# A Mamba-2 scan with a hash-routed expert layer: x in two transfers per sequence, y in natural order, C's parity masks on ScalarE, and a new order of the steps

## The chip, the cores and the metric

The kernel runs on one NeuronCore of a Trainium2 chip. Five engines take part: TensorE (PE, with its weight loads as PEld), VectorE (DVE), ScalarE (ACT), GpSimd (POOL) and SyncE (SP), which here only issues DMAs. The metric is the device time of one launch in microseconds. Before the change it was 355.7 us, the median of three runs (354.11 to 358.03).

## The reference

Two stages follow one another, all in float32.

The first is a state-space scan over 4 sequences, 8 heads, 768 steps, with 32 values per head (x) and a state of 16 (B and C). With `la = log(clip(a, 1e-6, 1))` and chunks of 32 steps:

```python
cum = np.cumsum(la, axis=-1)
L = np.exp(cum[:, :, :, None] - cum[:, :, None, :]) * causal
M = np.einsum('bhin,bhjn->bhij', Cc, Bc) * L
y = einsum('bhij,bhjd->bhid', M, xc) + einsum('bhin,bhnd->bhid', Cc, state) * exp(cum)
state = exp(sum(la)) * state + sum_j Bc_j xc_j exp(cum[-1] - cum_j)
```

The second takes the result as 3072 tokens of 256 values. A token's expert is `token_ids * 2654435761 % 8`; each expert computes `relu(x @ w1[e]) @ w2[e]` with a hidden width of 1024.

## The kernel before

**The scan.** A sequence is cut into 12 units of 64 steps; two units make a chunk of 128 steps, so there are 6 chunks per sequence and 24 in all (`gc` counts them, `b, c = divmod(gc, 6)`). `fac` holds exp(-cum) and exp(cum), with cum counted from the middle of a unit, for all four sequences.

For a sequence `b` the steps are these. `load_bc` and `load_x` read B, C and x. `rows(b, 0)` multiplies B by its factor and `rows(b, 1)` C by its own. `put_steps` stores the scaled B to a scratch tensor in HBM, and `get_steps` reads it back as the tile `bs` with steps on the partitions. `turn_b` and `turn_c` transpose the scaled B and C on PE, 96 rows at a time, into `bt` and `ct`; `turn_c` also makes `ce` (two copies of C, each with the heads of one parity masked to zero) and `cp` (C times the decay of a unit). `states` multiplies `bs` by x on PE and chains the units' states on DVE; `blocks` spreads the states into `up`. `grams` forms C·B for a chunk and multiplies it by the causal mask on DVE, giving `m`; `outputs` adds `cp`·`up` and `m`·x in PSUM, ACT copies the sum to `y_sb`, and SP stores it to `y_tokens` in HBM.

**What sets the order.** `tc.manual_schedule()` keeps each engine's instructions in the order of the code, so every engine, and SP as the queue of the loads and stores, works through one fixed list. Lines 490 to 504 are the prologue for sequence 0. In the loop of lines 506 to 541 chunk `gc` issues `grams(gc + 1)` and `outputs(gc)`, then one segment of `routing()` (a generator, advanced by `next(todo)`), and then a step for the next sequence `nb`, chosen by `c`:

```python
c == 0: rows(nb, 0), rows(nb, 1), load_x(nb + 1)
c == 1: put_steps(nb), turn_b(nb), load_bc(nb + 1)
c == 2: get_steps(nb), turn_c(nb)
c == 3: states(nb, 0)
c == 4: states(nb, 1), blocks(nb, 1, UH + 1)
c == 5: blocks(nb, UH + 1, NU)
```

**The routing.** Its first segment makes the expert ids from the token ids (`eid_i`, `eid_r`, a PE transpose), the second a one-hot mask and two PE matmuls that count tokens, the next three prefix sums; later ones build `at` and `of`, whose product on PE (`L346`, 24 matmuls) inverts the permutation into `idx_in` and `idx_out`.

**The expert stage.** After the last chunk GpSimd gathers token rows by `idx_in`, PE runs the eight experts, and GpSimd scatters the results.

**Buffers.** The pool `ps_t` has two PSUM tiles named `tp`, used by the transposes, `states`, the routing and `steps`; `ps_y` has one `y_ps`. `spin` is a run of matmuls whose result is not read. `aload` holds three `x_t` and one `bc`.

Of the kernel before, what the change touches and what calls it, by code (L numbers as in the profile page):

```python
# [20 lines left out]
def kernel(  # L21
# [65 lines left out]
    def load_bc(b):  # L87
        t = aload.tile([NR, 2, H, RS, NS], F32, name="bc", bufs=1)
        for i, src in ((0, B), (1, C)):
            nc.sync.dma_start(out=t[:, i].rearrange("p h r n -> p h (r n)"),  # L90
                              in_=src[b].rearrange("h (p r) n -> p h (r n)", r=RS))
        bcs[b] = t

    def load_x(b, parts=1):

        t = aload.tile([P, NU, G, D], F32, name="x_t", bufs=3)
        for u in range(parts):
            us = slice(u * NU // parts, (u + 1) * NU // parts)
            for h in range(H):
                q, k = divmod(h, G)  # L100
                nc.sync.dma_start(out=t[q * HL:(q + 1) * HL, us, k],  # L101
                                  in_=x[b, h].rearrange("(u j) d -> j u d", j=HL)[:, us])
        xs[b] = t

    load_bc(0)
# [3 lines left out]
    load_x(0, 2)  # L109
# [3 lines left out]
    def load_w(e):  # L113
# [10 lines left out]
    upto = const.tile([P, P], F32)  # L124
    nc.gpsimd.affine_select(out=upto, in_=ones, pattern=[[1, P]], compare_op=OP.is_ge,
                            fill=0.0, base=0, channel_multiplier=-1)
    causal = const.tile([P, 2 * G, RS, RU], F32)
    nc.gpsimd.memset(causal[0:HL], 1.0)
    nc.gpsimd.affine_select(out=causal[0:HL], in_=causal[0:HL], pattern=[[0, 2 * G], [1, RS], [RS, RU]],
                            compare_op=OP.is_ge, fill=0.0, base=0, channel_multiplier=-1)  # L130
    nc.gpsimd.tensor_copy(out=causal[HL:P], in_=causal[0:HL])
# [42 lines left out]
    nc.vector.tensor_scalar(out=a_t, in0=a_t, scalar1=1e-6, scalar2=1.0, op0=OP.max, op1=OP.min)  # L174
# [5 lines left out]
    tot = apre.tile([NR, BH], F32)  # L180
    nc.vector.tensor_copy(out=tot, in_=cum[:, :, RS - 1])
    rel_ps = ps_t.tile([P, 512], F32, name="tp")
    nc.tensor.matmul(out=rel_ps[0:NR, 0:BH], lhsT=rel_w.rearrange("p k r -> p (k r)"), rhs=tot, start=True, stop=True)
    off = apre.tile([NR, BH], F32)
    nc.vector.tensor_copy(out=off, in_=rel_ps[0:NR, 0:BH])
    nc.vector.tensor_tensor(out=cum, in0=cum, in1=off.unsqueeze(2).to_broadcast([NR, BH, RS]), op=OP.add)
    fac = apre.tile([NR, 2, BH, RS], F32)
    nc.scalar.activation(fac[:, 0], cum, AF.Exp, scale=-1.0)
    nc.scalar.activation(fac[:, 1], cum, AF.Exp)
# [5 lines left out]
    nc.gpsimd.tensor_copy(out=totx, in_=tot.unsqueeze(2).to_broadcast([NR, BH, NS]))  # L195

# [162 lines left out]

# [23 lines left out]
    def turned(b, i):  # L383
        t = rws.pop((b, i))
        for r0 in (0, RS // 2):
            tp = ps_t.tile([P, 512], F32, name="tp")
            v = tp[:, 0:RS // 2 * NR].rearrange("p (r c) -> p r c", c=NR)
            for r in range(RS // 2):
                nc.tensor.transpose(out=v[:, r], in_=t[:, r0 + r], identity=ident[0:NR, 0:NR])  # L389
            yield r0, v.rearrange("p r (k c) -> p r k c", c=RU)  # L390

    def turn_b(b):
        bt = abat.tile([P, NU, RU, RS], F32, name="bt")
        for r0, v in turned(b, 0):
            o = bt[:, :, :, r0:r0 + RS // 2].rearrange("p k c r -> p r k c")
            if b == 0 and r0:
                nc.vector.tensor_copy(out=o, in_=v)
            else:
                nc.scalar.activation(o, v, AF.Copy)
        bts[b] = bt  # L400

    def turn_c(b):
        ct = abat.tile([P, NU, RS, RU], F32, name="ct", bufs=1)
        for r0, v in turned(b, 1):
            nc.scalar.activation(ct[:, :, r0:r0 + RS // 2].rearrange("p k r c -> p r k c"), v, AF.Copy)
        ce = abat.tile([P, 2, NU, HL], F32, name="ce")
        c3 = ct.rearrange("p k r c -> p k (r c)")
        for e in range(2):
            nc.vector.tensor_scalar(out=ce[:, e], in0=c3, scalar1=par[:, e:e + 1], scalar2=None, op0=OP.mult)  # L409
        cp = abat.tile([P, NU, HL], F32, name="cp")  # L410
        nc.gpsimd.tensor_tensor(out=cp, in0=c3, in1=step[:, b].unsqueeze(2).to_broadcast([P, NU, HL]), op=OP.mult)
        ces[b], cps[b] = ce, cp

    def states(b, half):
# [6 lines left out]
        for i in range(n):  # L421
            k = half * UH + i
            for r in range(G):
# [3 lines left out]
                                 rhs=xb[w, k, 2 * g:2 * g + 2].rearrange("p h d -> p (h d)"), start=True, stop=True)  # L427
# [8 lines left out]
    def blocks(b, k0, k1):  # L436
# [4 lines left out]
        nc.gpsimd.tensor_tensor(out=ups[b][:, k0:k1], in0=sts[b][:, k0:k1].unsqueeze(2).to_broadcast(sh),  # L441
# [4 lines left out]
    def grams(gc):  # L446
# [3 lines left out]
        for u in range(2):  # L450
            for r in range(G):
# [3 lines left out]
                                 lhsT=bts[b][rr, 2 * c + u].rearrange("p c r -> p (c r)"), rhs=ces[b][rr, :, 2 * c + u],  # L455
# [3 lines left out]
                                in1=causal.rearrange("p (g x) r c -> p g (x r c)", g=2), op=OP.mult)  # L459
        ms[gc] = m  # L460

    def outputs(gc):
# [11 lines left out]
        for h in range(G):  # L474
            g, e = divmod(h, 2)
            for q in range(2):
                w = slice(q * HL, (q + 1) * HL)
                for u in range(2):
                    k = 2 * c + u
                    nc.tensor.matmul(out=y_ps[u * HL:(u + 1) * HL, q, h * D:(h + 1) * D], lhsT=m[w, g, u, e],  # L480
                                     rhs=xs[b][w, k, h], start=(k == 0 and h == 0), stop=(h == G - 1),
# [3 lines left out]
        for u in range(2):  # L485
            t0 = gc * P + u * HL
            nc.sync.dma_start(out=y_dram[t0:t0 + HL, :].rearrange("(p r) d -> r p d", r=RS),
# [235 lines left out]
```

## Time and profile before

| | us |
|---|---|
| median of 3 runs | 355.7 |
| the profiled execution | 356.14 |
| its span in the trace | 354.4 |
| PE busy | 287.9 (81%) |
| DVE busy | 111.6 (31%) |
| ACT busy | 49.4 (14%) |
| POOL busy | 110.0 (31%) |
| mean granted PE clock | 0.834 |

The profile is one execution; 1.74 us of its time lie outside the span. Times of single instructions are counted from the span's start. A busy PE is not PE at its peak: the granted clock says which of its two levels (1.2 and 2.4 GHz, 0.5 and 1.0) it ran at. The scan takes the first 127 us of the span, the gathers follow, and the expert stage runs from 142.8 us to the end.

### The profile page before, as it was taken

The page shows a single profiled execution, that of the slowest core. Times are in us where ns is not written, and L with a number is a line of the kernel's source. Part 1 is how long each engine was busy: PE and PEld are TensorE (multiplying, and loading weights), DVE is VectorE, ACT ScalarE, POOL GpSimd, SP SyncE. Part 2 cuts the span into 40 slices and gives each one's busy share as a digit, 9 for nine tenths or more (in the row PEclk, how much of TensorE's full clock was granted, in tenths as well). Part 3 has the DMA queues.
Part 4 walks back from the last instruction along what each step waited for, and adds up shares of the span by engine and source line. Part 5 has one row for each costly group of instructions (what it writes and reads, how often), then busy time and mean ns, then how long its engine had stood idle before and what let it go on. Part 6 is the DMA issues. An engine that isn't in the chain of part 4 may idle for free.

```text
span 354.4 us, 6033 instructions
## 1 busy us (share of the span) xinstructions
PE 287.9 (81%) x2461; PEld 182.5 (51%) x2461; DVE 111.6 (31%) x222; ACT 49.4 (14%) x101; POOL 110.0 (31%) x115
## 2 busy tenths in 40 slices
PE   6743789818777722999999999999999999999940
PEld 5533668617566620555555555555555555655510
DVE  2724359745958301111221221121222212211110
ACT  4200211300211010100110111111111111111110
POOL 8404315212616317413054052161350310201330
PEclk9855555656757885699999999999999999999985
DMA  8598841591944459403415324424210000100010
GB/s 129 104 158 114 191 95 30 99 213 35 297 109 151 147 157 372 154 10 129 147 44 167 118 74 140 135 78 168 99 59 5 30 14 0 46 0 15 33 35 14
DMA packets 58129, 36.45 MB, mean 103 GB/s; under 512 B 36559, under 2 KB 53993, under 8 KB 58100
## 3 DMA queue, kind: packets, MB, share of 16 engines
q1 hardware_dynamic: 55284, 29.49, 32.2%
q0 software_dynamic: 2816, 6.56, 5.7%
q8 instruction: 20, 0.33, 0.4%
q14 instruction: 9, 0.07, 0.1%
HBM read 28.17 MB, written 8.13 MB: 102 GB/s over the span
## 4 chain that ended last, share of the span: by engine, by line
PE 45%; issue 20%; DMA 14%; DVE 9%; POOL 5%; SPq 4%; ACT 1%; POOLq 0%; ACTq 0%; DVEq 0%
PE h_ps L595 16%; PE o_ps L604 15%; DMA out_dram<-o_sb,idx_out 6%; DMA bs<-b_steps 3%; DVE st L433 3%; POOL out_dram L565 3%; PE y_ps L480 2%; PE gram L454 2%; PE tp L426 2%; DMA xg<-y_tokens,idx_in 2%; SPq L101 2%; PE xt_ps L583 2%; DMA bc<-in_C_dram 2%; PE tp L389 1%; PE y_ps L471 1%
## 5 line engine op out<-in xcount | busy, mean ns | idle before, releaser
L595 PE MATMUL h_ps<-xT,w 128*128 128x416 f32 x256 | 102.3, 524 | 0.3 <-DVE xT L584 0.3
L604 PE MATMUL o_ps<-hT,w 128*128 128x416 f32 x256 | 102.1, 518 | 0.0
L604 PEld LDWEIGHTS o_ps<-hT,w 128*128 128x128 f32 x256 | 47.5, 190 | 40.1 <-issue 36.3
L565 POOL DMA_INDIRECT out_dram<-o_sb,idx_out x32 | 31.2, 974 | 114.1 <-ACT o_sb L626 95.8
L595 PEld LDWEIGHTS h_ps<-xT,w 128*128 128x128 f32 x256 | 47.4, 195 | 32.5 <-issue 30.8
L560 POOL DMA_INDIRECT xg<-y_tokens,idx_in x32 | 32.0, 1000 | 50.2 <-PE xt_ps L583 20.4
L590 DVE TENSOR_SCALAR hT<-h_ps 128x416 f32<-128x416 f32 x32 | 18.9, 592 | 74.8 <-PE h_ps L595 74.8
L584 DVE COPY xT<-xt_ps 128x256 f32<-128x256 f32 (+1 forms) x32 | 12.0, 375 | 77.6 <-PE xt_ps L583 77.6
L588 ACT ACTIVATE hT<-h_ps 128x416 f32<-128x416 f32 x32 | 16.6, 517 | 100.6 <-PE h_ps L595 100.6
L426 PE MATMUL tp<-x_t,bs 64*32 64x64 f32 x352 | 13.3, 308 | 17.0 <-issue 10.4
L441 POOL TENSOR_TENSOR up<-st,own 128x768 f32<-128x768 f32 (+1 forms) x8 | 13.4, 1672 | 44.2 <-DVE st L433 44.2
L454 PE MATMUL gram<-ce,bt 32*64 32x128 f32 x384 | 23.3, 379 | 2.2 <-DVE ce L409 2.2
L480 PE MATMUL y_ps<-x_t,m 64*64 64x32 f32 x768 | 21.4, 257 | 4.2 <-DVE m L458 4.2
L480 PEld LDWEIGHTS y_ps<-x_t,m 64*64 64x64 f32 x768 | 21.6, 184 | 5.1 <-DVE m L458 5.1
L583 PE MATMUL xt_ps<-ident,xg 128*128 128x128 f32 (+1 forms) x64 | 12.6, 280 | 13.0 <-DMA xg<-y_tokens,idx_in 12.0
L583 PEld LDWEIGHTS xt_ps<-ident,xg 128*128 128x128 f32 (+1 forms) x64 | 8.4, 147 | 26.2 <-issue 23.0
L484 ACT ACTIVATE y_sb<-y_ps 128x256 f32<-128x256 f32 x24 | 9.2, 384 | 89.5 <-PE y_ps L480 86.2
L458 DVE TENSOR_TENSOR m<-gram,causal 128x512 f32<-128x512 f32 x24 | 16.4, 685 | 16.4 <-PE gram L454 16.4
L426 PEld LDWEIGHTS tp<-x_t,bs 64*32 64x32 f32 x352 | 10.6, 164 | 18.7 <-issue 16.4
L454 PEld LDWEIGHTS gram<-ce,bt 32*64 32x64 f32 x384 | 15.0, 184 | 5.3 <-DVE ce L409 2.4
L471 PE MATMUL y_ps<-up,cp 64*64 64x128 f32 x176 | 14.4, 384 | 3.4 <-POOL up L441 2.7
L626 ACT ACTIVATE o_sb<-ot_ps 128x256 f32<-128x256 f32 x16 | 6.1, 384 | 60.2 <-PE ot_ps L623 60.2
(121 smaller groups left out, 192.8 us busy)
## 6 DMA issues: line engine op xcount, KB each, us to landing
w<-in_moe_w_dram SPq DMA_DIRECT2D x16, 1024.0 KB
y_tokens<-y_sb SPq DMA_DIRECT2D x48, 64.0 KB
x_t<-in_x_dram SPq DMA_DIRECT2D x24, 96.0 KB
bc<-in_B_dram SPq DMA_DIRECT2D x4, 384.0 KB
bc<-in_C_dram SPq DMA_DIRECT2D x4, 384.0 KB
b_steps<-rows SPq DMA_DIRECT2D x4, 384.0 KB
bs<-b_steps SPq DMA_DIRECT2D x8, 192.0 KB
x_t<-in_x_dram SPq DMA_DIRECT2D x16, 48.0 KB
```

The lines of the kernel that those rows point to most:

```text
L426: nc.tensor.matmul(out=tp[32 * r:32 * r + 32, i * PW:(i + 1) * PW], lhsT=bs[w, k, 32 * g:32 * g + 32], rhs=xb[w, k, 2 * g:2 * g + 2].rearr ...
L454: nc.tensor.matmul(out=gram[q * HL:(q + 1) * HL, g, u * P:(u + 1) * P], lhsT=bts[b][rr, 2 * c + u].rearrange("p c r -> p (c r)"), rhs=ces[ ...
L458: nc.vector.tensor_tensor(out=m.rearrange("p g u e i -> p g (u e i)"), in0=gram[:, :, 0:2 * P], in1=causal.rearrange("p (g x) r c -> p g ( ...
L471: nc.tensor.matmul(out=y_ps[u * HL:(u + 1) * HL, q, 0:P], lhsT=cps[b][w, k], rhs=ups[b][w, k].rearrange("p g x -> p (g x)"), start=True, s ...
L480: nc.tensor.matmul(out=y_ps[u * HL:(u + 1) * HL, q, h * D:(h + 1) * D], lhsT=m[w, g, u, e], rhs=xs[b][w, k, h], start=(k == 0 and h == 0), ...
L560: nc.gpsimd.indirect_dma_start(out=dst, out_offset=None, in_=y_dram[:], in_offset=bass.IndirectOffsetOnAxis(ap=idx, axis=0), bounds_check= ...
L565: st = nc.gpsimd.indirect_dma_start(out=out[:], out_offset=bass.IndirectOffsetOnAxis(ap=idx, axis=0), in_=src, in_offset=None, bounds_chec ...
L583: nc.tensor.transpose(out=tp[:, i, 0:r], in_=g[0:r, i * P:(i + 1) * P], identity=ident[0:r, 0:r])
L588: nc.scalar.activation(o, i, AF.Relu)
L590: nc.vector.tensor_scalar_max(out=o, in0=i, scalar1=0.0)
L595: nc.tensor.matmul(out=hp, lhsT=w1s[e][:, i, f * P:(f + 1) * P], rhs=xT[e][:, i], start=(i == 0), stop=(i == DP - 1))
L604: nc.tensor.matmul(out=oP[e][:, j, 0:CAP], lhsT=w2s[e][:, f, j * P:(j + 1) * P], rhs=h, start=(f == 0), stop=(f == FP - 1))
```

## The change

- `load_x` issues two transfers per sequence, one for each group of four heads, instead of 8 (16 for sequence 0), and the tile's free dimensions are `[head, unit, value]` instead of `[unit, head, value]`. The runs of contiguous bytes stay 32 floats long.
- The transposes write PSUM as `(column, row)`, so that `bt`, `ct`, `ce` and `causal` hold a unit's 64 steps in natural order; `outputs` stores a chunk with one transfer of 128 rows instead of two of 64 permuted rows.
- `turn_c` makes `ce` with four ScalarE activations per sequence, each with a scale per partition, straight from PSUM; the two DVE multiplications go.
- In the prologue: `tok` is loaded before B and C; `upto` and `causal` are built on GpSimd after `totx`; `tot` is a view and not a copy; `rel` is added straight from PSUM; the first five segments of `routing()` are issued before chunk 0; `rows(0, 1)`, `cp` and the first state block of sequence 0 are on DVE; `grams(0)` stands ahead of the spins.
- In the loop: `put_steps` moves from `c == 1` to `c == 0`, `get_steps` from `c == 2` to `c == 1`; `load_bc` moves to `c == 0`, `load_x` to `c == 1`, behind `get_steps`; `blocks` follow their `states` directly.

```diff
 def load_bc(b):
-    t = aload.tile([NR, 2, H, RS, NS], F32, name="bc", bufs=1)
+    t = aload.tile([NR, 2, H, RS, NS], F32, name="bc")
...
-def load_x(b, parts=1):
-    t = aload.tile([P, NU, G, D], F32, name="x_t", bufs=3)
-    for u in range(parts):
-        us = slice(u * NU // parts, (u + 1) * NU // parts)
-        for h in range(H):
-            q, k = divmod(h, G)
-            nc.sync.dma_start(out=t[q * HL:(q + 1) * HL, us, k],
-                              in_=x[b, h].rearrange("(u j) d -> j u d", j=HL)[:, us])
+def load_x(b):
+    t = aload.tile([P, G, NU, D], F32, name="x_t", bufs=3)
+    for q in range(2):
+        nc.sync.dma_start(out=t[q * HL:(q + 1) * HL].rearrange("j h k d -> j (h k) d"),
+                          in_=x[b, q * G:(q + 1) * G].rearrange("h s d -> (h s) d").rearrange("(c j) d -> j c d", j=HL))
...
 def turned(b, i):
...
-        v = tp[:, 0:RS // 2 * NR].rearrange("p (r c) -> p r c", c=NR)
+        v = tp[:, 0:RS // 2 * NR].rearrange("p (c r) -> p c r", r=RS // 2)
         for r in range(RS // 2):
-            nc.tensor.transpose(out=v[:, r], in_=t[:, r0 + r], identity=ident[0:NR, 0:NR])
+            nc.tensor.transpose(out=v[:, :, r], in_=t[:, r0 + r], identity=ident[0:NR, 0:NR])
...
-def turn_c(b):
-    ct = abat.tile([P, NU, RS, RU], F32, name="ct", bufs=1)
-    for r0, v in turned(b, 1):
-        nc.scalar.activation(ct[:, :, r0:r0 + RS // 2].rearrange("p k r c -> p r k c"), v, AF.Copy)
-    ce = abat.tile([P, 2, NU, HL], F32, name="ce")
-    c3 = ct.rearrange("p k r c -> p k (r c)")
-    for e in range(2):
-        nc.vector.tensor_scalar(out=ce[:, e], in0=c3, scalar1=par[:, e:e + 1], scalar2=None, op0=OP.mult)
+def turn_c(b, eng):
+    ct = abat.tile([P, NR, RS], F32, name="ct", bufs=1)
+    ce = abat.tile([P, 2, NR, RS], F32, name="ce")
+    for rs, v in turned(b, 1):
+        for e in range(2):
+            nc.scalar.activation(ce[:, e, :, rs], v, AF.Identity, scale=par[:, e:e + 1])
+        nc.scalar.activation(ct[:, :, rs], v, AF.Copy)
...
-        for u in range(2):
-            t0 = gc * P + u * HL
-            nc.sync.dma_start(out=y_dram[t0:t0 + HL, :].rearrange("(p r) d -> r p d", r=RS),
-                              in_=y_sb[u * HL:(u + 1) * HL].rearrange("p q d -> p (q d)"))
+        nc.sync.dma_start(out=y_dram[gc * P:(gc + 1) * P, :], in_=y_sb.rearrange("p q d -> p (q d)"))
...
+todo = iter(routing())
+next(todo)
 rows(0, 0, nc.vector)
 put_steps(0)
+rows(0, 1, nc.vector)
+heads()
 get_steps(0)
-rows(0, 1, nc.gpsimd)
-heads()
+load_bc(1)
+load_x(1)
 turn_b(0)
 steps()
+next(todo)
+turn_c(0, nc.vector)
+grams(0)
 spin(ones, 2)
-load_bc(1)
-turn_c(0)
+next(todo)
+next(todo)
+next(todo)
 spin(ones, 4)
-grams(0)
 states(0, 0)
-blocks(0, 1, UH + 1)
-load_x(1)
-todo = iter(routing())
+blocks(0, 1, 2, nc.vector)
+blocks(0, 2, UH + 1, nc.gpsimd)
...
         if c == 0:
             rows(nb, 0, nc.gpsimd)
             rows(nb, 1, nc.gpsimd)
+            put_steps(nb)
+            if nb + 1 < NB:
+                load_bc(nb + 1)
+        elif c == 1:
+            turn_b(nb)
+            get_steps(nb)
             if nb + 1 < NB:
                 load_x(nb + 1)
-        elif c == 1:
-            put_steps(nb)
-            turn_b(nb)
-            if nb + 1 < NB:
-                load_bc(nb + 1)
         elif c == 2:
-            get_steps(nb)
-            turn_c(nb)
+            turn_c(nb, nc.gpsimd)
         elif c == 3:
             states(nb, 0)
+            blocks(nb, 1, UH + 1, nc.gpsimd)
         elif c == 4:
             states(nb, 1)
-            blocks(nb, 1, UH + 1)
+            blocks(nb, UH + 1, NU, nc.gpsimd)
```

SP's list from the first chunks of sequence 1 on, where sequence 2 is prepared; before:

```order
L487 DMA y_tokens<-y_sb 8x8x256 x4
L101 DMA x_t<-in_x_dram 64x12x32 x8
L487 DMA y_tokens<-y_sb 8x8x256 x2
L373 DMA b_steps<-rows 96x1024
L90 DMA bc<-in_B_dram 96x8x128
L90 DMA bc<-in_C_dram 96x8x128
L487 DMA y_tokens<-y_sb 8x8x256 x2
L379 DMA bs<-b_steps 64x12x64 x2
```

And after:

```order
L477 DMA y_tokens<-y_sb 128x256 x2
L368 DMA b_steps<-rows 96x1024
L90 DMA bc<-in_B_dram 96x8x128
L90 DMA bc<-in_C_dram 96x8x128
L477 DMA y_tokens<-y_sb 128x256
L374 DMA bs<-b_steps 64x12x64 x2
L98 DMA x_t<-in_x_dram 64x48x32 x2
```

The eight x transfers that stood ahead of the store and the two reads of the scaled B now stand behind them, as two, and B and C of the following sequence still lie between the store and the reads.

PE's list in the prologue (`L168`/`L157` are the spins, `L389`/`L385` the transposes, `L426`/`L418` the states); before:

```order
L389 MATMUL tp<-ident,rows 128x96 x8
L200 MATMUL tp<-step_w,totx 128x12 x4
L168 MATMUL y_ps<-ones,ident 128x128 x2
L389 MATMUL tp<-ident,rows 128x96 x8
L168 MATMUL y_ps<-ones,ident 128x128 x4
L454 MATMUL gram<-ce,bt 64x128 x8
L426 MATMUL tp<-x_t,bs 32x64 x24
```

And after:

```order
L239 MATMUL tp<-ident,eid_r 128x24
L385 MATMUL tp<-ident,rows 128x96 x8
L196 MATMUL tp<-step_w,totx 128x12 x4
L250 MATMUL tp<-mask,ones 128x192
L251 MATMUL tp<-mask,upto 128x192
L385 MATMUL tp<-ident,rows 128x96 x8
L446 MATMUL gram<-ce,bt 64x128 x8
L157 MATMUL y_ps<-ones,ident 128x128 x6
L418 MATMUL tp<-x_t,bs 32x64 x24
```

The routing's three matmuls now come before the first states, and all six spins directly ahead of them.

DVE's list around the first `rows`; before:

```order
L186 TENSOR_TENSOR cum<-cum,off 96x256
L223 CAST iota_b<-iota_c 128x53
L368 TENSOR_TENSOR rows<-bc,fac 96x8x8x16
L209 TENSOR_REDUCE par<-hm 128x2
L210 TENSOR_TENSOR hm<-hm 128x4
```

And after:

```order
L174 TENSOR_TENSOR rel<-cum,tp 96x256
L219 CAST iota_b<-iota_c 128x53
L235 TENSOR_SCALAR eid_i<-tok 24x128
L237 CAST eid_r<-eid_i 24x128
L363 TENSOR_TENSOR rows<-bc,fac 96x8x8x16 x2
L205 TENSOR_REDUCE par<-hm 128x2
```

The scaled B still stands behind `iota_b`, which waits for GpSimd's `iota_c`, and now behind the two expert-id instructions too.

## Rows read from the trace of the kernel before

**Rows 1.** Stages: length, busy us of PE, PEld, DVE, ACT, POOL, clock, DMA share, GB/s

```profile
30.10:59.20 29.10, 21.86 (x433) 18.12 (x437) 16.43 (x38) 4.62 (x9) 9.05 (x6) 0.50 0.54 113
59.20:88.40 29.20, 19.00 (x440) 15.72 (x444) 17.56 (x35) 4.85 (x10) 8.13 (x5) 0.59 0.53 108
88.40:111.60 23.20, 18.88 (x440) 15.31 (x440) 18.70 (x26) 4.75 (x10) 9.05 (x6) 0.63 0.55 164
111.60:127.20 15.60, 11.12 (x340) 9.20 (x340) 5.77 (x15) 2.30 (x6) 6.95 (x3) 0.89 0.53 177
127.20:354.40 227.20, 200.18 (x640) 109.62 (x640) 41.33 (x88) 27.22 (x57) 63.15 (x64) 0.94 0.26 86
```

**Rows 2.** Waits of PE from 23 to 128 us: total, times, longest

```profile
PE tp L426 <- issue: 10.4, 3, 8.2
PE y_ps L480 <- DVE m L458: 4.2, 3, 2.0
PE tp L346 <- POOL of L342: 3.1, 1, 3.1
PE tp L426 <- DMA bs<-b_steps: 2.9, 4, 1.4
```

**Rows 3.** Timeline of SP: start, length, what, count

```profile
4.18 11.05 SPq L101 DMA_DIRECT2D x_t<-in_x_dram  x16
...
63.51 6.39 SPq L101 DMA_DIRECT2D x_t<-in_x_dram  x8
...
75.02 1.44 SPq L379 DMA_DIRECT2D bs<-b_steps  x2
```

**Rows 4.** The chain of waits up to 31 us, and its last store: start, length, what

```profile
2.90 5.68 DMA bc<-in_C_dram
...
15.34 3.19 DMA b_steps<-rows
...
23.19 1.60 PE tp L426 x44
...
26.70 1.81 POOL up L441
...
127.68 0.57 SPq L487
```

**Rows 5.** Three short stretches, columns as in group 1

```profile
10.00:12.00 2.00, 1.77 (x10) 1.34 (x8) 1.95 (x3) 0.82 (x1) 1.71 (x1) 0.60 0.46 73
24.00:28.00 4.00, 1.83 (x43) 1.26 (x34) 2.23 (x7) 0.00 (x0) 1.30 (x1) 0.50 1.44 168
38.60:40.25 1.65, 1.62 (x6) 1.56 (x7) 0.00 (x0) 0.00 (x0) 0.00 (x0) 0.50 0.59 115
```

**Rows 6.** Timeline of DVE in the prologue: start, length, what, [idle before]

```profile
8.60 0.20 DVE L223 CAST iota_b<-iota_c 128x53 bf16<-128x53 f32 x1 [0.84 <-POOL iota_c L221]
8.70 1.22 DVE L368 TENSOR_TENSOR rows<-bc,fac 96x1024 f32<-96x1024 f32 x1
```

**Rows 7.** Groups of instructions by line: busy us, mean ns, idle before

```profile
L409 DVE TENSOR_SCALAR ce<-ct,par 128x768 f32<-128x768 f32 x8 | 9.8, 1269 | 7.5 <-ACT ct L405 7.5
L399 ACT ACTIVATE bt<-tp 128x384 f32<-128x384 f32 x7 | 5.7, 876 | 7.1 <-PE tp L389 7.1
L405 ACT ACTIVATE ct<-tp 128x384 f32<-128x384 f32 x8 | 3.7, 490 | 2.5 <-PE tp L389 2.3
```

**Rows 8.** The chain of waits from 60 us on: one chunk and a transpose

```profile
68.67 1.47 PE tp L389 x8
70.14 1.06 PE gram L454 x16
71.20 0.64 PE y_ps L471 x8
71.84 0.84 PE y_ps L480 x32
```

**Rows 9.** Timeline of POOL: `rows` of sequence 2

```profile
60.23 3.82 POOL L368 TENSOR_TENSOR rows<-bc,fac 96x1024 f32<-96x1024 f32 x2
```

## What was predicted

> **What bounds the kernel now.** I read the busy time by stages first, then what PE waited for, then the chain of waits with SP's and DVE's timelines at the places it names.
>
> The stages [rows 1] split the span in two. From 127.2 us on (gathers and experts, 227.2 us) PE works 200.18 us at a mean clock of 0.94, and the change edits nothing there but the store just ahead of it. Everything else lies in the first 127.2 us, where PE is the engine with most work but stands idle: 7.24 us of 29.10 in chunks 1 to 5 (30.1 to 59.2), 10.20 of 29.20 for sequence 1, 4.32 of 23.20 for sequence 2 and 4.48 of 15.60 for the last. Its clock is granted at 0.50 to 0.63 until 111.6 us, so mostly at 1.2 GHz.
>
> What PE waits for [rows 2]: 10.4 us before `states` where no releaser is named, 8.2 of them in one piece, and 2.9 us for `bs` by name. The large piece is `bs` too: its two reads were issued only at 75.02, behind eight x transfers that held SP from 63.51 for 6.39 us [rows 3]. Then come DVE late with `m` (4.2) and GpSimd late with the routing's mask products (3.1).
>
> The prologue's chain is B's round trip through HBM [rows 4]: SP issued sixteen x transfers from 4.18 to 15.23 [rows 3]; only then, at 15.34, came the store of the scaled B, though DVE had it ready at 8.70 + 1.22 = 9.92 [rows 6]; it landed at 18.53, and the states began at 23.19, so 4.66 us for the reads.
>
> **The sum, stage by stage,** against the profiled execution (356.14 us, 0.44 over the median of 355.7).
>
> *Up to the first states, 23.19 before.* Two chains race. The DMA chain: with two transfers SP is free after about 1.3 us of issuing, and x goes at the queue's pace. While x was issued piece by piece the DMA engines were 0.46 busy at 73 GB/s; with B, C and x queued together full at 168 GB/s [rows 5]. At 73 / 0.46 = 159 to 168 GB/s the 786 KB take 4.7 to 5.0 us; behind C, which landed at 2.90 + 5.68 = 8.58 [rows 4], they end near 13.6. `iota_b`, which waits for GpSimd's `iota_c` [rows 6], comes later than 8.60, since GpSimd now waits for `cum` with that work still ahead; I take 1.2 us, and with the two expert-id instructions the scaled B is ready near 11.6, covered by x. Its store then lands near 16.3 (3.19 less the issue that the queue covers), `bs` near 20.9. The compute chain is longer now. From 11.6: transposes of B (1.47 if at 1.2 GHz [rows 8], 0.9 at 2.4), two ACT copies in between, since the routing holds the other PSUM tile, `steps`, the counting matmuls (1.62 [rows 5]), C's first four transposes, three ACT operations, the other four, two more, `gram` (1.06), six spins (1.8 to 2.6). ACT operations on 384 elements cost 490 ns written in runs of 8 floats and 876 written one by one [rows 7]; the new ones write runs of 4, nearer the first, so I take 0.55. This sums to between 21.3 and 24.2; I take 22.6: **-0.6** (-1.9 to +1.0).
>
> *First chunk.* GpSimd's block of six units, 1.81 us [rows 4], is on the path from the states to the first y. Now DVE does the one unit needed (a sixth of the elements, about 0.2): **-1.6**. The rest runs beside chunk 0.
>
> *Chunks 1 to 5.* Idle was 7.24 us; the counting matmuls (1.62 [rows 5]) leave this stretch. New waits: after chunk 0, `turn_b(1)` needs GpSimd to finish five units (1.5) and the first half of `rows` (1.9 of 3.82 [rows 9]) behind the second states (1.3 PE, 1.6 DVE): 6.3 us, of which PE fills 3.8 with work, so 2.5 idle. `bs(1)` comes 3.19 + 4.66 us after that [rows 4], 7.9, against 1.47 + 2.54 + 1.47 + 2.54 = 8.0 us of PE work [rows 8]; B and C of sequence 2 (786 KB) lie ahead in the queue and can add up to 4.7; between 0 and 4.6 I take 0.5, since they have those 7.9 us to move in. -7.24 - 1.62 + 2.5 + 0.5 = **-5.9**.
>
> *Chunks 6 to 23.* Idle 10.20 + 4.32 + 4.48 = 19.0 us. The `bs` waits go: for sequence 2 `put_steps` leaves as soon as GpSimd has made it, and `bs` arrives about 1.6 (DVE) + 1.5 (GpSimd's block) + 1.9 + 3.2 + 4.7 = 13 us after the previous sequence's last states, against the five chunks and two transposes that PE does meanwhile, 5 x 2.54 + 2 x 1.47 = 15.6 us at 1.2 GHz [rows 8]; B and C in the queue could make it up to 17.7. I leave DVE's 4.2 in: two mask multiplications of 1269 ns per sequence go [rows 7], but the routing's instructions on DVE remain. GpSimd's products (0 to 3.1 [rows 2]) I take at 1.4, about half, since they still stand right behind `rows`. 19.0 - 5.6 = **-13.4**.
>
> *Last store.* One y transfer instead of two: **-0.6** (0.57 [rows 4]).
>
> Sum: -22.1, so 334.0. **Clock:** chunks 1 to 5 had 433 matmuls in 21.86 us of PE at 0.50, the last sequence 340 in 11.12 at 0.89 [rows 1]: 50 against 33 ns each. With the gaps gone some of it should be granted 2.4 GHz. It can't all pay: at that clock the 13 us chain of `bs` plus about 3 us of PE (both `states` and a chunk) is the limit of a sequence, 16 against 19.0 us of PE work now, so 0 to -3 on two sequences. I take -2 in all: **332 us**.
>
> Costed at nothing: x's new tile layout (runs of 32 floats as before), the prologue's other trims (0.2 us each, hidden behind the round trip), the second `bc` buffer (4.32 us idle hides a late load), y's natural order.
>
> **A rule against it: masks on ScalarE.** The rows give 2.54 us of DVE per sequence for the masks, against four more ACT operations of 0.49 to 0.88, 2.0 to 3.5 us [rows 7]. In the loop `y_sb` of the next chunk now stands behind six of them, about 4.2 us from the first transpose; PE needs the PSUM tile back 6.5 us after it at 1.2 GHz, so nothing is lost there. Only the prologue has them on its path, as counted. The Trainium skill, ScalarE: Activation LUTs, Rules for kernel authors, says to give multiplications to VectorE and not to ScalarE. From that page's cost of an activation (186 ns + 0.833 per element, 93 per pointer operand) my estimate is 0.6 us for each mask, which would make the sum 0.2 us longer. What hangs on the rule is thus the prologue alone.
>
> **Rivals.**
>
> 1. *Forecast, 332*: 0.55.
> 2. *`bs` stays late.* For: B and C precede it in one queue, for two of three sequences. The waits of 0.5 and 0 become 4.6 and 17.7 - 15.6 = 2.1: 332 + 6 = 338. Against: the time they have to move in. 0.18.
> 3. *The clock rises for good.* Then two sequences fall to the chain's 16 us (-6) and chunks 2 to 5 to 33 ns per matmul (about -3): 332 + 2 - 9 = 325. For: from about 34 us on I see no wait left over 2 us. Against: chunks 1 to 5 had PE busy for three quarters of the time and were granted 0.50 [rows 1]. 0.13.
> 4. *x is not faster.* If x keeps 73 GB/s in two transfers, it ends at 8.6 + 10.8 = 19.4, and the states start 7.3 later, at 26.7: 332 + 4 = 336. Against: a share of 0.46 is a queue that lacked work [rows 5]. The Trainium skill, DMA: Bandwidth & Descriptors, Specifications, asks for pieces of at least 512 B, and x's stay at 128 B. By that rule larger transfers alone would not help; the trace shows x at 168 GB/s beside others. 0.06.
> 5. *Slower: the transposes' strided writes.* Each transpose now writes PSUM in steps of 16 bytes, which no row shows. Eight take 1.47 us [rows 8], 64 of them 11.8. They stand in PE's list between chunks, so every added ns counts. From 2.9 times on the gain of 22 is gone; at four times, 332 + 35 = 367. Against: ACT's rows show a factor under 2 for its own strided writes. 0.04.
>
> The last 0.04: several gains fail at once, 346 to 356.
>
> Range: the low end joins rival 3 with a prologue of 21.3, 325 - 1.3; the high end takes rivals 2 and 4 together with 1.0 more in the prologue, 343. **323 to 343.** Measurement tells about 1% here (the runs spread 354.11 to 358.03), so 3.6 us: faster by more than that 0.92, within it 0.04, slower 0.04.
>
> **What would show it.** SP: x as two issues, the first `b_steps` store before 13 us; the states at 21 to 24 with `ce` on ACT, not `bs`, released last. PE: no wait over 2 us before `states` in the loop, one of about 2.5 before `turn_b(1)`; chunk 5 ending near 51, chunk 23 near 103. `L385` transposes at 1.5 us for eight. ACT's masks near 0.55 us. Wrong if `states` still waits several us for `bs`, if transposes or masks are twice as long, or if the stretch behind the last y changes by more than 1 us.

## The result, and the profile after

The changed kernel takes **345.19 us** (median of 4 runs, 344.89 to 346.07) against 355.25 for the kernel before on the same chip (354.11 to 358.03): a ratio of 0.971, 95% interval 0.965 to 0.9769. It is faster, by 10 us. The forecast was 332 with a range of 323 to 343, so the sign was right, and of the 24 us less than half came. On another chip, with six runs, the ratio was 0.973 (0.9671 to 0.9788).

The profiled execution took 344.89 us (span 343.2, mean clock 0.843), 11.25 less than the profiled one of before. Its stages, cut at the same events as [rows 1] and in the same columns (first states to first y, chunks 1 to 5, sequence 1, sequence 2, the last sequence, the rest):

```profile
25.05:29.65 4.60, 3.24 (x105) 2.82 (x108) 2.49 (x9) 0.00 (x0) 1.13 (x1) 0.78 0.81 69
29.65:52.40 22.75, 17.19 (x429) 14.35 (x432) 15.40 (x29) 5.65 (x13) 9.01 (x6) 0.62 0.78 135
52.40:72.10 19.70, 16.97 (x440) 13.92 (x441) 14.54 (x27) 6.03 (x14) 8.91 (x5) 0.74 0.91 161
72.10:101.20 29.10, 20.80 (x466) 17.41 (x464) 14.81 (x30) 6.14 (x14) 16.31 (x7) 0.59 0.43 129
101.20:117.40 16.20, 10.48 (x320) 8.83 (x316) 4.20 (x7) 2.30 (x6) 1.54 (x1) 0.74 0.54 182
117.40:343.20 225.80, 199.55 (x640) 109.34 (x640) 41.23 (x88) 27.19 (x57) 63.17 (x64) 0.93 0.26 86
```

Chunks 1 to 5 fell from 29.1 to 22.75 us and sequence 1 from 29.2 to 19.7, as hoped. But sequence 2 *grew* from 23.2 to 29.1 and the last from 15.6 to 16.2: 5.9 and 0.6 us given back. The prologue grew too, by 1.86 us (states at 25.05, was 23.19). What PE waits for up to 145 us (total, times, longest), the same kind of row as [rows 2], which covers 23 to 128 us:

```profile
PE xt_ps L578 <- DMA xg<-y_tokens,idx_in: 11.1, 2, 10.1
PE y_ps L463 <- ACT y_sb L476: 6.1, 3, 5.1
PE tp L342 <- POOL of L338: 4.8, 1, 4.8
PE y_ps L472 <- DVE m L450: 4.0, 3, 1.9
PE tp L385 <- POOL rows L363: 3.8, 1, 3.8
PE tp L385 <- ACT ct L400: 3.0, 2, 1.5
```

The first line is the wait for the gathers behind the scan, which stood before too (12.0 us). The 8.2 us wait for `bs` is gone. The longest waits of the scan are now two that [rows 2] had small or not at all: 4.8 us for GpSimd's mask products (it was 3.1), and 5.1 us for `y_sb`, which was none of the four largest.

**The wait for `y_sb`.** The chain of waits (start, length, what) passes through it:

```profile
101.34 0.39 ACT y_sb L476
101.75 9.03 DMA y_tokens<-y_sb
110.78 0.02 issue
...
110.89 0.39 ACT y_sb L476
...
111.32 0.71 PE y_ps L463 x8
```

One y store of 128 KB, median 3.1 us to landing, took 9.03. SP's timeline shows what stands ahead of it:

```profile
100.43 0.38 SPq L112 DMA_DIRECT2D w<-in_moe_w_dram  x1
100.88 0.45 SPq L114 DMA_DIRECT2D w<-in_moe_w_dram  x1
101.75 14.41 SPq L477 DMA_DIRECT2D y_tokens<-y_sb  x6
```

These are expert 1's weights, 2 MB in two transfers (`load_w(1)`), the second issued less than 1 us before the store. `y_sb` has three buffers; three chunks on, ACT can't write and PE stands for 5.09 us. Before, SP issued the same two from 110.28 on, and PE then waited for GpSimd's products anyway (3.1 us, [rows 2]):

```profile
110.28 0.44 SPq L115 DMA_DIRECT2D w<-in_moe_w_dram  x1
```

So the load was covered by a stall, and the change moved the stall away; e2 tests this.

**GpSimd's products**, in its timeline (start, length, what), stand behind `rows`:

```profile
75.94 5.77 POOL L363 TENSOR_TENSOR rows<-bc,fac 96x1024 f32<-96x1024 f32 x2
81.68 2.30 POOL L336 TENSOR_TENSOR of<-of,iota_b 128x1272 bf16<-128x1272 bf16 x1
83.97 3.50 POOL L338 TENSOR_SCALAR of<-of,one_up 128x1272 bf16<-128x1272 bf16 x1
```

PE's list came to the routing's product (L346 before, now L342) at 82.7 and could start it at 87.52. Before, the same two stood elsewhere, in POOL's timeline of the kernel before:

```profile
90.36 3.90 POOL L368 TENSOR_TENSOR rows<-bc,fac 96x1024 f32<-96x1024 f32 x2
...
111.23 2.31 POOL L340 TENSOR_TENSOR of<-of,iota_b 128x1272 bf16<-128x1272 bf16 x1 [1.42 <-DVE of L337]
```

They ran in chunk 18, behind DVE and 21 us after the last `rows` had begun. Since five of the routing's segments are now issued in the prologue, the products have moved to chunk 14. The two `rows` of this sequence took 5.77 us, those in [rows 9] 3.82. Behind that wait `turn_c` ran with only one `tp` tile and waited 1.52 us more for `ct`.

**The prologue**, PE's timeline (start, length, what, [idle before]):

```profile
16.30 0.85 PE L385 MATMUL tp<-ident,rows 96*128 96x96 f32 x4
18.66 0.90 PE L385 MATMUL tp<-ident,rows 96*128 96x96 f32 x4 [1.52 <-ACT ct L400]
20.71 1.13 PE L446 MATMUL gram<-ce,bt 32*64 32x128 f32 x16 [1.14 <-ACT ce L399]
21.77 3.35 PE L157 MATMUL y_ps<-ones,ident 128*128 128x128 f32 x12
25.05 1.51 PE L418 MATMUL tp<-x_t,bs 64*32 64x64 f32 x48
```

No DMA releases the states: they stand behind six spins, 3.35 us at the low clock. From 11.11 to 25.05 the granted clock was 0.50 throughout; before, it was 0.81 from 10 to 14.3 us and 0.73 from there to the states.

### The profile page after: what moved, and what is told of

Read it like the earlier page. It is cut to its first block, busy times and chain, and to the rows that moved or that the text cites. A ratio compares the mean times of both kernels' runs of the same rounds, so it can differ in the third digit from the quotient of the medians.

```text
span 343.2 us, 5958 instructions
## 1 busy us (share of the span) xinstructions
PE 285.7 (83%) x2461; PEld 181.5 (53%) x2461; DVE 102.2 (30%) x214; ACT 55.1 (16%) x118; POOL 106.5 (31%) x113
## 4 chain that ended last, share of the span: by engine, by line
PE 47%; issue 20%; DMA 15%; POOL 9%; DVE 5%; ACT 2%; POOLq 0%; SPq 0%; ACTq 0%; DVEq 0%
PE h_ps L590 17%; PE o_ps L599 15%; DMA out_dram<-o_sb,idx_out 6%; DMA y_tokens<-y_sb 3%; POOL out_dram L560 3%; PE tp L385 2%; PE y_ps L472 2%; PE gram L446 2%; PE tp L418 2%; DMA xg<-y_tokens,idx_in 2%; DMA bs<-b_steps 2%; PE xt_ps L578 2%; POOL rows L363 2%; DVE st L425 2%; PE y_ps L463 1%
## 5 line engine op out<-in xcount | busy, mean ns | idle before, releaser
L583 ACT ACTIVATE hT<-h_ps 128x416 f32<-128x416 f32 x32 | 16.5, 517 | 98.9 <-PE h_ps L590 98.9
L433 POOL TENSOR_TENSOR up<-st,own 128x640 f32<-128x640 f32 (+1 forms) x8 | 13.1, 1641 | 36.3 <-DVE st L425 36.3
L472 PE MATMUL y_ps<-x_t,m 64*64 64x32 f32 x768 | 20.7, 257 | 4.0 <-DVE m L450 4.0
L472 PEld LDWEIGHTS y_ps<-x_t,m 64*64 64x64 f32 x768 | 20.9, 184 | 4.8 <-DVE m L450 4.7
L446 PE MATMUL gram<-ce,bt 32*64 32x128 f32 x384 | 21.4, 353 | 1.1 <-ACT ce L399 1.1
L463 PE MATMUL y_ps<-up,cp 64*64 64x128 f32 x176 | 13.8, 376 | 7.6 <-ACT y_sb L476 6.1
L385 PE MATMUL tp<-ident,rows 96*128 96x96 f32 x64 | 13.0, 373 | 8.4 <-POOL rows L363 3.8
L446 PEld LDWEIGHTS gram<-ce,bt 32*64 32x64 f32 x384 | 13.8, 172 | 4.2 <-issue 2.0
L385 PEld LDWEIGHTS tp<-ident,rows 96*128 96x128 f32 x64 | 10.1, 221 | 9.9 <-POOL rows L363 4.1
```

Source lines behind the costliest of these rows:

```text
L385: nc.tensor.transpose(out=v[:, :, r], in_=t[:, r0 + r], identity=ident[0:NR, 0:NR])
L446: nc.tensor.matmul(out=gram[q * HL:(q + 1) * HL, g, u * P:(u + 1) * P], lhsT=bts[b][rr, 2 * c + u], rhs=ces[b][rr, :, 2 * c + u], start=Tr ...
L463: nc.tensor.matmul(out=y_ps[u * HL:(u + 1) * HL, q, 0:P], lhsT=cps[b][w, k], rhs=ups[b][w, k].rearrange("p g x -> p (g x)"), start=True, s ...
L583: nc.scalar.activation(o, i, AF.Relu)
```

## Experiments

All ratios are to the kernel before, run beside it on the same chip. The edits of e1 to e4, e6, e9 and e10 are to the changed kernel.

### e1: six y_sb buffers

```diff
-        y_sb = awork.tile([P, 2, P], F32, name="y_sb")
+        y_sb = awork.tile([P, 2, P], F32, name="y_sb", bufs=6)
```

> The changed kernel with six y_sb buffers instead of three; nothing else. Theory: in the changed kernel PE waited 5.1 us before chunk 21 because y_sb was full, and it was full because the stores of chunks 17 and later lie behind 2 MB of the second expert's weights in one queue. With six buffers the stores are as late as before (about 9 us to landing for chunk 17), but ACT and PE don't wait: chunks 21 to 23 keep 2.4 GHz, 1.44 us each instead of 2.5. The last y then ends 5 to 8 us earlier, 337 to 340 us. Rival: the single 128-row store is slow by itself, or the gathers only wait longer for late stores; then the time stays at 345 (343 to 346), with the wait moved behind the last y.

Measured: 340.84 us, ratio 0.9601 (0.9509 to 0.9692), between the theory's 340 and the rival's 343. One store still took 8.8 us to land, but the wait for `y_sb` fell to 0.5 us, so the stores' landing was what PE had waited for. Yet 3.12 us of standing came back at the same place with no releaser, in PE's timeline:

```profile
105.88 0.44 PE L463 MATMUL y_ps<-up,cp 64*64 64x128 f32 x5
109.44 0.32 PE L463 MATMUL y_ps<-up,cp 64*64 64x128 f32 x2 [3.12 <-issue]
```

PE stopped in the middle of a group of eight matmuls. In that stretch (105 to 110 us) the queues carried, beside the load, one packet of the instruction queue (packets, MB, share of 16 engines):

```profile
q1 hardware_dynamic: 1142, 1.07, 62.5%
q8 instruction: 1, 0.02, 1.2%
```

That PE's instructions themselves wait behind the load fits this; it was not measured by itself.

### e2: the load earlier

```diff
-            elif b == 2:
-                load_w(1)
...
             if nb + 1 < NB:
                 load_x(nb + 1)
+            else:
+                load_w(1)
```

> The changed kernel with the second expert's weights (2 MB) issued at chunk 13, behind the last get_steps, instead of at chunk 16. Theory (weights ahead of the y stores): they move while PE waits for the routing's products anyway, the wait of 5.1 us before chunk 21 goes and the clock stays at 2.4 GHz: 337 to 340 us. Rival (the store itself is slow): stores still take about 9 us and the wait stays, 344 to 346 us. If the weights now hold up something else, it is the stores of chunks 13 to 15, with a wait of up to 3 us before chunk 16: 340 to 343 us.

Measured: 337.3 us, ratio 0.9523 (0.9435 to 0.9611). Now both transfers move while PE waits for the products:

```profile
PE tp L342 <- POOL of L338: 5.9, 1, 5.9
...
PE y_ps L463 <- ACT y_sb L476: 0.6, 1, 0.6
```

The 5.1 us are gone, and chunks 21 to 23, 2.1 to 2.5 us each in the changed kernel behind the wait, take 1.44. The forecast of 337 to 340 held. This is the largest single item, 7.9 us.

### e3: the products three chunks later

```diff
-        else:
+        elif gc not in (14, 15, 16):
             next(todo, None)
```

> The changed kernel with the routing held for three chunks (14 to 16), so that the inverse product on PE comes after chunk 17 and not after chunk 14. Theory: PE waited 4.8 us there for GpSimd's mask products, which stand right behind rows of sequence 3, and 1.5 us more because the product's PSUM tile made turn_c serial; both go, and 1 to 2 us come back as a wait for bs: 4 to 6 us faster than the changed kernel, 339 to 341 us, if the wait behind the weights before chunk 21 stays as it is. Rival: the chain of rows, store, reads and states of sequence 3 is the limit there, so the time freed is spent waiting for bs: 343 to 346 us.

Measured: 340.26 us, ratio 0.9593 (0.9515 to 0.9672), as expected. The wait for the products and the one for `ct` behind it (3.0 in two, now 1.5 in one) are gone, and from ACT's copy of chunk 14 to that of chunk 18 it took 15.0 us instead of 20.1. The condition that the wait behind the weights stays did not hold: in place of 5.1 us for `y_sb` PE stood 2.3 us under the name "issue".

### e4: no spins ahead of the states

```diff
-    spin(ones, 2)
...
-    spin(ones, 4)
```

> The changed kernel without the six spins ahead of the first states (their result is not read). Theory: the first states start at 25.1 us because of them (3.3 us at 1.2 GHz behind gram, which ended at 21.8), while bs has long landed: states at 21.9, and nearly all of it is kept because the first sequence runs on chains of DVE, GpSimd and DMA: 2 to 3.5 us faster than the changed kernel, 342 to 343 us. Rival: bs lands only shortly before 25 us, or the clock they keep up is worth as much as they cost: 344.5 to 347 us.

Measured: 342.77 us, ratio 0.965 (0.9562 to 0.9738), in the theory's 342 to 343, but not parted from the changed kernel, whose interval is 0.965 to 0.9769. In the trace the states begin at 21.46 instead of 25.05. Of these 3.6 us, 1.4 return at once, as the wait for DVE's `up` grows:

```profile
21.46 1.51 PE L418 MATMUL tp<-x_t,bs 64*32 64x64 f32 x48
22.89 1.13 PE L446 MATMUL gram<-ce,bt 32*64 32x128 f32 x16
26.76 0.48 PE L463 MATMUL y_ps<-up,cp 64*64 64x128 f32 x2 [2.74 <-DVE up L433]
```

The rest is gone one chunk later. The changed kernel was granted 0.78 from its states to the first y and 1.00 over chunk 1, e4 0.50 over both. The last matmuls of chunk 1, first in e4, then in the changed kernel:

```profile
30.95 1.02 PE L472 MATMUL y_ps<-x_t,m 64*64 64x32 f32 x32
```

```profile
31.14 0.62 PE L472 MATMUL y_ps<-x_t,m 64*64 64x32 f32 x32
```

This is the mechanism of the rival (a clock worth as much as the spins cost). But the spins do not secure that clock: e2 has them and was granted 0.53 over chunk 1. So what they cost in the whole is not shown.

### e5, e6, e7: together, and the load cut up

e5 has the edits of e2, e3 and e4. e6 cuts `load_w(1)` into eight pieces of 256 KB; e7 is e6 with the edits of e3 and e4.

```diff
-            elif b == 2:
-                load_w(1)
...
+        if 13 <= gc <= 20:
+            part_w(1, gc - 13)
```

> The three single edits together (weights of expert 1 loaded at chunk 13, the mask products three chunks later, no spins). If their gains add up: 345.2 - 7.9 - 4.9 - 2.4 = 330.0 us (328.5 to 331.5). Rival: the 2 MB load costs PE about 5 us wherever PE has work to do; at chunk 13 it was free only because PE stood waiting 5.9 us for GpSimd's mask products there, and those are now later. Then 334 to 336 us, with a wait of 2 to 5 us in chunks 14 to 18, named y_sb or issue.

> The changed kernel with the weights of expert 1 loaded in eight pieces of 256 KB, one behind the y store of each chunk from 13 to 20. Theory (a y store, or PE's own instructions, wait behind 2 MB at once): no piece holds the queue longer than about 0.8 us, so the 5.1 us wait before chunk 21 goes and the last chunks run at 2.4 GHz: 336 to 339 us. Rival (it is the load as such that slows the chunks beside it, however cut): 342 to 345 us, with the wait spread over several chunks.

> The cut load with the mask products three chunks later and no spins. Theory: nothing is left of the three waits, 328 to 331 us, at or below the kernel with the load in one piece at chunk 13. Rival (a load beside working PE always costs): 334 to 336 us.

Measured: e5 334.04 us, ratio 0.9384 (0.9331 to 0.9438); e6 337.0, 0.9476 (0.9423 to 0.953); e7 330.74, 0.9318 (0.925 to 0.9386).

e6 supports the cause: five of its eight pieces, issued from 100.08 on, moved beside the same chunks as the 2 MB had, and it lost nothing that e2 saved. Its theory held. Its first pieces left three chunks earlier, however, so cutting is not parted from starting sooner. e5 came out at its rival's 334 to 336, but not by the rival's mechanism: no wait named `y_sb` or "issue" is over 0.6 us. What differs from e7 in the profiled executions is PE's clock. From 76.1 us to the end of chunk 16 e5 needed 17.70 us for as many matmuls as e7 did in 13.80 (the columns are those of the stages, the clock third from the right). First e5, then e7:

```profile
76.10:93.80 17.70, 14.46 (x296) 11.83 (x292) 8.29 (x13) 5.24 (x13) 13.70 (x7) 0.54 0.85 269
```

```profile
76.10:89.90 13.80, 10.19 (x296) 8.27 (x296) 6.94 (x12) 5.04 (x13) 12.42 (x6) 0.87 0.73 226
```

Cause or chance? The e7 kernel, run again as e14 on another chip, had 0.61 over the same chunks, which took it 16.5 us, and the ratio 0.9418. So cutting the load brings nothing measurable over an early load, and the clock of this stretch is not fixed by the program.

### e8: the kernel before with the new loop order alone

```diff
             rows(nb, 1, nc.gpsimd)
-            if nb + 1 < NB:
-                load_x(nb + 1)
+            put_steps(nb)
+            if nb + 1 < NB:
+                load_bc(nb + 1)
         elif c == 1:
-            put_steps(nb)
             turn_b(nb)
+            get_steps(nb)
...
+                load_x(nb + 1)
```

The rest of the edit is `blocks` at c == 3 and 4 and a second `bc` buffer.

> The kernel before with the loop's order of the changed one alone (B stored at c = 0, read at c = 1 ahead of the x loads, blocks at c = 3 and 4, two bc buffers); x still in eight transfers, two y stores per chunk, masks on DVE, the old prologue. Theory: the 8.2 us wait for bs in sequence 1 goes here too, and GpSimd's products and the 2 MB load then become waits of PE just as they did in the changed kernel, so of 8.2 + 2.9 about half stays: 349 to 351 us; the rest of the change's 10 us is prologue and first chunk. Rival A: the order is the whole gain, 344 to 347 us. Rival B: eight x issues behind the reads hold SP for 3 us per sequence and delay y stores, nothing is gained: 354 to 357 us.

Measured: 349.44 us, ratio 0.9833 (0.9767 to 0.9899), within the theory's 349 to 351. PE's waits:

```profile
PE y_ps L480 <- DVE m L458: 8.6, 5, 3.7
PE tp L346 <- POOL of L342: 6.1, 1, 6.1
...
PE tp L426 <- DMA bs<-b_steps: 1.7, 2, 1.1
```

The order alone takes most of the `bs` waits away (under the name "issue" 1.5 us are left of 10.4), and the same products become the new wait (3.1 to 6.1). That half of the theory is seen; a wait on the load is not: it was issued at 99.76, and PE stood in those 6.1 us from 103.4 to 109.5. The waits for DVE's `m` double (4.2 to 8.6). The order alone thus gives 5.6 us, beside the 10 of the change.

### e9 and e10: x in eight transfers; masks on DVE

```diff
-        for q in range(2):
-            nc.sync.dma_start(out=t[q * HL:(q + 1) * HL].rearrange("j h k d -> j (h k) d"),
...
+        for h in range(H):
+            q, k = divmod(h, G)
+            nc.sync.dma_start(out=t[q * HL:(q + 1) * HL, k], in_=x[b, h].rearrange("(u j) d -> j u d", j=HL))
```

```diff
-            for e in range(2):
-                nc.scalar.activation(ce[:, e, :, rs], v, AF.Identity, scale=par[:, e:e + 1])
             nc.scalar.activation(ct[:, :, rs], v, AF.Copy)
+        for e in range(2):
+            nc.vector.tensor_scalar(out=ce[:, e], in0=ct, scalar1=par[:, e:e + 1], scalar2=None, op0=OP.mult)
```

> The changed kernel with x in eight transfers per sequence, one for each head, instead of two (tile layout and order kept). Theory (two large transfers are no cheaper for SP: they took it 5.10 us in the prologue and 5.45 in the loop, and eight took 6.39 before, some 0.7 to 0.8 each): the number of x transfers is worth little, what counted was the order; 344.5 to 347.5 us, first states at 25 to 26 us. Rival (fewer transfers carry the gain of the prologue and of the sequences): 349 to 353 us, states 2 us or more later.

> The changed kernel with C's parity masks on DVE again, as two multiplications of the whole ct per sequence; ACT copies ct alone. Theory (ACT's masks relieve DVE, which is late with m in the loop): DVE's 2 x 1.27 us per sequence come back, its waits (4.0 us before y) grow to 6 or more, states(0,0) about 0.5 us later: 346 to 350 us. Rival (masks belong on VectorE; ACT's six operations per sequence held the PSUM tile and made PE wait 3.0 us for ct): those waits go, 342 to 344.5 us.

Measured: e9 343.81 us, ratio 0.9573 (0.9516 to 0.9629), states at 24.89; e10 343.46, 0.9588 (0.9535 to 0.9642), states at 24.55. For e9 theory and rival asked for 344.5 us or more, and neither would have it lower; of the theory it stands that the number of transfers is worth little. e10 has the rival's number, but half its mechanism: the wait for `ct` shrank from 3.0 to 1.2 us, and the one for DVE's `m` stayed at 4.0, where the theory wanted 6. The kernel before took 357.69 us on that chip, 2.4 more than on the first, which by itself makes both ratios lower.

### e11: B and C of the next sequence behind the reads

e7 with this edit:

```diff
             put_steps(nb)
-            if nb + 1 < NB:
-                load_bc(nb + 1)
         elif c == 1:
             turn_b(nb)
             get_steps(nb)
             if nb + 1 < NB:
+                load_bc(nb + 1)
                 load_x(nb + 1)
```

> The kernel with cut load, late mask products and no spins, and load_bc of the sequence after next issued behind the two reads of bs instead of ahead of them. PE waits for bs there 1.4, 3.2 and 2.4 us at the start of states. Theory (B and C, 786 KB, stand ahead of the reads in the queue): the two waits in sequences 0 and 1 fall by 3 us or more together, 327 to 329 us against 330.7; the third, which has no load_bc, stays near 2.4. Rival (the round trip itself, GpSimd's product, store and read, is the length): waits within 1 us of what they were, 330 to 331.5 us.

Measured: 335.02 us, ratio 0.9329 (0.9269 to 0.9389), against 0.9318 for e7 on another chip: no gain is seen, though the intervals are as wide as the 1% that the theory asked for. The waits for `bs` in the first two sequences did go (1.4 and 3.2 us), and the third stayed (2.4 in e7, 2.7 here). PE's timeline shows two stops that e7's does not have, and the third wait:

```profile
72.42 0.65 PE L457 MATMUL gram<-ce,bt 32*64 32x128 f32 x11 [3.35 <-issue]
84.05 0.71 PE L474 MATMUL y_ps<-up,cp 64*64 64x128 f32 x8 [2.17 <-ACT y_sb L487]
88.27 0.42 PE L429 MATMUL tp<-x_t,bs 64*32 64x64 f32 x4 [2.71 <-DMA bs<-b_steps]
```

The first has no releaser; B, C and x, now issued in one block, were moving in it. In the second, ACT waits for a y store issued behind the 2 MB of expert 0, which left at 73.15 (70.90 in e7). The theory was right on the wait and, as far as these runs tell, wrong on the time; that the block holds up what comes next fits, but was not isolated.

### e12, e13, e14: on one chip

e12 is the changed kernel, e14 the kernel of e7, e13 that with e10's edit.

> The changed kernel as it is, on one chip with the two next: 345 us in the terms of the first chip, ratio 0.968 to 0.975 to the kernel before. If masks and x transfers gained nothing (theory), the kernels with DVE masks (0.9588) and with eight x transfers (0.9573) stay 1% or more below it or equal to it; if their ratios were only another chip's, the changed kernel itself comes out at 0.957 to 0.960 here.

> The kernel with cut load, late mask products and no spins, and with C's masks on DVE. Theory (each mask on ACT costs the prologue 0.5 us and the loop the wait for ct; DVE has room): 1 to 3 us below the same kernel with ACT masks in this call. Rival (with the other waits gone DVE's m is what PE waits for next, and 2.5 us per sequence on DVE come back): 1 to 4 us above it.

> The kernel with cut load, late mask products and no spins as run before, masks on ACT, as the partner of the one with DVE masks on the same chip: ratio 0.925 to 0.939 to the kernel before, and 4% (13 to 16 us) under the changed kernel.

Measured: e12 344.87 us, ratio 0.973 (0.9671 to 0.9788); e14 333.46, 0.9418 (0.9354 to 0.9482); e13 334.95, 0.9421 (0.9348 to 0.9494). e13 and e14 can't be told apart: neither the theory nor the rival is borne out, and where the masks are made does not matter to the time of this kernel. e12 kept its ratio on a third chip. That does not explain the 1.2 to 1.4% by which e9 and e10 were lower, for it did not run on theirs; in microseconds the single runs overlap (341.3 to 345.3 against 342.9 to 346.7); a small gain from undoing either can't be excluded, a loss is not seen.

## Why the prediction missed

Stage by stage, forecast against measured change (us):

| step | forecast | measured |
|---|---|---|
| up to the first states | -0.6 | +1.9 |
| first chunk | -1.6 | -2.3 |
| chunks 1 to 5 | -5.9 | -6.4 |
| chunks 6 to 23 | -13.4 | -3.0 (-9.5, +5.9, +0.6) |
| last store and after | -0.6 | -1.4 |
| clock | -2 | within the stages |

**The step that failed is chunks 6 to 23**: "Idle 10.20 + 4.32 + 4.48 = 19.0 us ... -13.4". It summed the waits that the change removes and left in only DVE's 4.2 and half of GpSimd's, 5.6 us, and it is 10.4 us off. Measured are 16.75 us of idle time (2.73 + 8.30 + 5.72): 6.1 for `y_sb`, 4.8 for the products, 4.0 for `m`, 1.5 for `ct`. PE's work there took nearly as long as before (48.25 us, 49.00 before).

- *GpSimd's products*: "I take at 1.4, about half, since they still stand right behind `rows`", bounds 0 to 3.1. They cost 4.8, and 1.5 for the `ct` wait. The "still" was wrong: they stood far behind `rows` before, and come right behind it only now, so the wait of before was no bound for the new place. There it is the length of GpSimd's list from 74.44 on (1.54 + 5.77 + 2.30 + 3.50 us) less what PE has to do meanwhile, and `rows` took 1.95 us more than in [rows 9]. e3 gives 4.9 us for them.
- *The weights' load*: it had no term and no rival. The last sequence was booked as idle time to be won, and I never asked what its transfers ran beside. e2 gives 7.9 us: 5.1 of waiting, and chunks at 2.1 to 2.5 us instead of 1.44 behind it.

Taken one by one these are 12.8 us, about the miss (345.2 - 332 = 13.2). They overlap, however: with both mended and the spins gone (2.4 alone, not parted from nothing) the gain was 11.2 us in e5, 14.5 in e7 and 11.4 in e14 (344.87 - 333.46, on one chip), not 15.2, with the granted clock making the difference between e5 and e7.

**The prologue**, sized 22.6 and found 25.05: not by a DMA, as the chain of [rows 4] was, but by PE's own list. The transposes began at 11.11, earlier than my 11.6, and the waits for ACT around C's second half (1.52 + 1.14 us) were in the sum. But I took 22.6 between 21.3 and 24.2, and all of it ran at the low clock, so the upper end applied. Beyond that, the spins took 3.35 us where I had 1.8 to 2.6, and the four matmuls of `steps`, to which I gave no price, 1.77. My bound of +1.0 was too small by 0.9. I also had SP free after 1.3 us of issuing x; it took 5.10, from 3.82 to 8.92, which cost nothing, as B's store left only at 10.99. I had named `ce` on ACT as the last to release the states; PE's own spins were.

**Chunks 1 to 5** came out near (-5.9, -6.4) in part by luck. Their idle time fell only to 5.56 us where the sum left 3.0: the wait of `turn_b(1)` was 3.8 and not 2.5, that for `bs(1)` 1.8 and not 0.5. The clock made up for it: 0.62 instead of 0.50, and PE busy for 17.19 us instead of 21.86, of which only 1.62 are the counting matmuls.

**The stretch behind the last y** shrank by 1.4 us, more than the 1 us that I had named as a sign of being wrong. Of this, 1.1 us lies ahead of the first gather (4.43 before, 3.33 now), nearly twice what one store less was put at, and 0.6 in the first expert matmuls, at a clock of 0.68 instead of 0.62; the gathers gave 0.3 back.

**Right by mechanism and size**: DVE's waits for `m` (4.2; 4.0), the first chunk's block on DVE, x not being the limit, and the transposes: eight with strided PSUM writes took 1.5 us as in [rows 8], so the slower rival had no ground. The masks:

```profile
L399 ACT ACTIVATE ce<-tp,par 128x384 f32<-128x384 f32 x16 | 8.4, 581 | 12.0 <-PE tp L385 12.0
L400 ACT ACTIVATE ct<-tp 128x384 f32<-128x384 f32 x8 | 4.0, 496 | 0.0
L391 ACT ACTIVATE bt<-tp 128x384 f32<-128x384 f32 x8 | 3.9, 490 | 10.7 <-PE tp L385 10.3
```

0.55 forecast, 0.581 measured; `bt` fell from 876 [rows 7] to 490 ns, unnoticed by the total. The rule that I cited from the Trainium skill, ScalarE: Activation LUTs, Rules for kernel authors (multiplications to VectorE), is borne out where I said it hung, in the prologue: from C's first transpose to `gram` it took 4.41 us with the masks on ACT and 4.10 in e10, 0.3 less. The states' start does not show it (24.55 in e10, but 24.50 in e12 with the masks on ACT), nor does the total.

**The rivals.** None was what cost the 13 us. *`bs` stays late* came nearest, and a single execution hides it. PE's waits for `bs` in the profiled execution, and in e12, the same kernel on another chip:

```profile
PE tp L418 <- DMA bs<-b_steps: 1.8, 2, 1.4
```

```profile
PE tp L418 <- DMA bs<-b_steps: 6.3, 4, 3.2
```

The second is about what the rival priced (4.6 + 2.1), and e1 to e4 and e6 have 5.8 to 7.1. Yet e12 took no longer (342.88 us profiled, against 344.89): PE had 1.00 of its clock in the chunks before (52.5 to 61.9 us; 0.76 from 52.4 to 62.7 in the other), came to the states of sequence 2 sooner and waited there. So the chain of `bs` limits what the clock can give, as the prediction argued, and e11 shows that taking this wait away does not by itself win its price.

The lowest times are those of e7, 0.9318 and 0.9418 of before on two chips, with e5 between them (0.9384): early or cut weights, late products, no spins.

## What to carry to other kernels

Before booking an idle stretch as gain, list what else moves in it: a transfer or an engine's late work covered by that stall becomes the next wait, and the price is read from what it takes by itself, not from how long PE waited before. A bulk load in the same queue as small stores that free buffers is best placed inside a wait that stays, or cut into pieces no longer than a step. And when an operation changes its place in an engine's list, its old wait bounds nothing: add up what stands ahead of it there.

## What was not expected of the hardware

- A 128 KB store behind 2 MB in one queue landed after 9.03 us, with a median of 3.1.
- PE stood 2.3 to 3.4 us with no releaser in the middle of a group of matmuls in e1, e3, e9 and e11, while large loads were in flight. One packet of the instruction queue moved in each of these stretches or just as it began, but one also moved between 100 and 104 us in the changed kernel, where PE did not stand; not isolated.
- The same kernel was granted 0.87 on one chip and 0.61 on another over the same chunks, which took 13.8 and 16.5 us (e7, e14).
- Two GpSimd products of the same shape took 5.77 us in one sequence and 3.82 in another, in both executions of the changed kernel; the cause is open.
- Two x transfers took SP 5.10 us to issue, eight took 7.04: here a transfer of four times the size took SP three times as long to issue.
